# A state-space layer and a gated feed-forward on one core: when one tile is split, when four scalings run, and how two blocks of results are stored

## The chip, the core and the metric

The kernel runs on one core of one Trainium2 chip. The core's engines each work through a queue of their own: TensorE (PE; its weight loads are listed as PEld), VectorE (DVE), ScalarE (ACT), GpSimd (POOL) and SyncE (SP), which here does nothing but issue transfers. ACT issues a few transfers as well. Engines wait for each other by semaphores, and each works strictly in its queue's order. The metric is the device time of one launch in microseconds (us); less is better. Before the change it is 934.74 us (median of three runs, 934.41 to 935.01).

## The reference

Input `A_u` is x, 2048 tokens by 640 channels. A modulation vector gives two triples of shift, scale and gate. The first half adds a gated long convolution (a diagonal state-space layer, 128 states for each channel) of the normalized x; the second half adds a gated SwiGLU feed-forward with 1728 hidden units. Cut to the part that the change touches:

```
mod = (silu(c) @ w_mod).reshape(1, 6, 1, 640)
sa, ca, ga, sb, cb, gb = ...                     # shift, scale, gate, twice
x = x + ga * ssm(layernorm(x) * (1 + ca) + sa)   # first 480 us or so of the kernel
h = layernorm(x) * (1 + cb) + sb
x = x + gb * ((silu(h @ w1) * (h @ w3)) @ w2)    # the rest
```

Everything is fp32. The kernel multiplies in TensorE with operands that are split into a high part (rounded) and a low part (the remainder), three products for one: high by high, high by low, low by high.

## The kernel before

**Tiles.** The tokens are four blocks of 512 (b = 0 to 3), a token's place in a block being a partition and one of four columns j. The hidden units are fourteen tiles m of 128; tile 13 has only 64, and is handled as 64 rows of high part with 64 rows of low part below them in one operand. `self.H` is the order in which the late stretches take the tiles: 13, 0, 1, ..., 12.

**Stages of the feed-forward.** Blocks are worked in pairs, p = 0 (blocks 0 and 1) and p = 1 (blocks 2 and 3). `groups(p, ...)` makes, for each tile m, gate and up projections of both blocks with a scheme that saves one product in eight, the SiLU gate, and for the even block at once the down projection (`down`, L968), added up in five PSUM banks `acc0` to `acc4`. The odd block's hidden tiles stay in SBUF, in `self.h`. `late(p, ...)` then follows: it finishes the even block (b = 2p) and runs the down projection of the odd block (b = 2p + 1) over all fourteen tiles, 15 matmuls of 512 columns for each (10 for tile 13).

**What a tile of `late` needs.** Its down weights `w` (high and low, 640 KB) come by SP from the scratch tensor `w2d` (L750) into three buffers, so the load for a tile can be issued only when the tile three places earlier is done with. Its hidden tile is split by `hidden_split` (L820): ACT copies the high part to `ah` (L601), DVE subtracts it for the low part `al` (L602), two buffers of each. PE takes high products first, and meets `al` as the third matmul of a tile.

**The even block's end.** ACT reads the five banks to `oc` (`gated`, L991). For k = 0 to 3 DVE multiplies each `oc` with the row of gates `gbrow` (L1002) and adds it to x (`token_add`, L1013); for k = 4 PE turns it to tokens (`to`) and DVE adds it (L1009). Then SP stores the block in four transfers of 320 KB, one for each 32 partitions (`store`, L1021). The calls are spread over the loop by the table `extra` (`at(...)`), but the tile framework's scheduler, which simulates the program as it builds it, decides in which order instructions stand in each engine's queue.

**Between the pairs.** At the end of `late(0)`, `plain(2, ...)` and `plain(3, ...)` make hidden tile 13 of blocks 2 and 3: products in bank `gh`, then ACT (tanh `th` L956, copy L957) and DVE (L958, and L959 that reads the bank for the last time). Block 2's tile, `aa`, is split at once inside `plain` (ACT L828 and L829, DVE L830, result `ah`); it is the first operand that the next group's down projection takes. Block 3's goes to `self.h`. The first group of p = 1 needs PSUM banks out of the same three (`gu`), which `to` and the second `gh` still hold.

**The end.** In `late(1)` the last two tiles are taken bank by bank. DVE multiplies (L1511) and adds (L1013) row by row, and `store_row` (L1015) stores each finished row j of block 3 in four transfers of 80 KB, two from SP and two from ACT.

Of the kernel before, what the change touches and what calls it, by code (L numbers as in the profile page):

```python
# [10 lines left out]
F32 = mybir.dt.float32  # L11
F32R = mybir.dt.float32r
I32 = mybir.dt.int32
AF = mybir.ActivationFunctionType
ALU = mybir.AluOpType
# [5 lines left out]
D = 640  # L21
# [184 lines left out]
class K:  # L206
# [392 lines left out]

    def split(self, H, Lo, v, eng):  # L600
        self.nc.scalar.activation(H, v, AF.Copy)  # L601
        eng.tensor_tensor(Lo, v, H.bitcast(F32), op=ALU.subtract)  # L602

    def bank(self, name):
        return self.ps.tile([P, 512], F32, name=name, tag="gu", bufs=3)
# [211 lines left out]
        i = self.H.index(m)  # L817
        return self.xp.tile([P, 512], F32, name=f"h{m}", tag="ha", bufs=4) if i >= 10 else self.fp.tile([P, 512], F32, name=f"h{m}", tag="hb", bufs=10)

    def hidden_split(self, b, m, a, eng):  # L820

        A = self.nc.scalar
        ah, al = (self.fp.tile([P, 512], F32R, name=f"a{x}{b}_{m}", tag=f"a{x}", bufs=2) for x in "hl")
        if m < 13:
            self.split(ah, al, a, eng)
            return ah, al
        th = self.tmp(f"t{b}_{m}")
        A.activation(ah[:64], a[64:], AF.Copy)  # L828
        A.activation(th[64:], ah[:64].bitcast(F32), AF.Copy)  # L829
        self.nc.vector.tensor_sub(ah[64:], a[64:], th[64:])  # L830
        return ah, None
# [99 lines left out]
    def plain(self, b, X, tiles):  # L931

        nc = self.nc
        A, V = nc.scalar, nc.vector
        out = []
        gu = []
        for f, W in tiles:
            if f == 13:
                gu.append((f, [(self.bank(f"gh{b}"), lambda k, W=W: [t[:, k % 2] for t in W[k // 2]])]))
            else:  # L940
                gu.append((f, [(self.bank(f"gu{b}{i}"), lambda k, i=i, W=W: [t[:, i if k == 4 else k % 2] for t in W[4 if k == 4 else 2 * i + k // 2]]) for i in range(2)]))
        for k in range(KT):
            x = list(self.x_of(X, b, k))
            for _, pg in gu:
                for g, w in pg:
                    self.three(g, w(k), x, k == 0, k == KT - 1)
        for f, pg in gu:
            th = self.tmp(f"th{b}{f}")
            g = pg[0][0]
            a = self.tmp(f"aa{b}{f}") if b % 2 == 0 else self.h_tile(f)  # L950
            if f < 13:
                A.activation(th, g, AF.Tanh, scale=0.5)
                V.scalar_tensor_tensor(a, th, 1.0, g, op0=ALU.add, op1=ALU.mult)
                V.tensor_mul(a, a, pg[1][0])
            else:
                A.activation(th[64:], g[:64], AF.Tanh, scale=0.5)  # L956
                A.activation(a[64:], g[:64], AF.Copy)  # L957
                V.scalar_tensor_tensor(a[64:], th[64:], 1.0, a[64:], op0=ALU.add, op1=ALU.mult)  # L958
                V.tensor_mul(a[64:], a[64:], g[64:])  # L959
            if b % 2:  # L960
                self.h[f] = a
            else:
                out.append(self.hidden_split(b, f, a, V))
        return out

    def accumulators(self, b):
# [2 lines left out]
    def down(self, acc, m, a, w, start, stop, ks=range(KT)):  # L969

        (ah, al), (w2h, w2l) = a, w
        wide, rest = slice(0, 4 * P), slice(4 * P, D)
        for k in ks:
            sl = slice(k * P, (k + 1) * P)
            terms = [(ah, w2h), (ah, w2l), (al, w2h)][:3 if m < 13 else 2]
            for i, (x, y) in enumerate(terms):
                last = stop and i == len(terms) - 1
                if k < 4:
                    self.pe.matmul(acc[k], x[:, sl], y[:, wide], start=start and i == 0, stop=last)
                else:  # L980
                    self.pe.matmul(acc[k], y[:, rest], x, start=start and i == 0, stop=last)

    def gate_row(self):

# [11 lines left out]
            self.nc.scalar.activation(oc, acc[k], AF.Identity, scale=self.cols[:, 2, k:k + 1])  # L996
        return oc

    def output(self, b, oc, k):

        if k < 4:
            self.nc.vector.tensor_mul(oc, oc, self.gbrow)  # L1002
            self.token_add(b, oc, k)
            return
        pt = self.bank(f"to{b}{k}")
        for j in range(4):
            self.pe.transpose(pt[:, j * P:(j + 1) * P], oc[:, j * P:(j + 1) * P], self.ident)
        xs = self.x2[b][:, :, k * P:(k + 1) * P]
        self.nc.vector.tensor_add(xs, pt.rearrange("p (j d) -> p j d", j=4), xs)  # L1009
# [3 lines left out]
        self.nc.vector.tensor_add(xs, oc, xs)  # L1013

    def store_row(self, b, j):  # L1015
        for q in range(4):
            (self.nc.scalar if q % 2 else self.nc.sync).dma_start(self.ov[q, :, b * 4 + j, :], self.x2[b][q * 32:(q + 1) * 32, j, :])

    def store(self, b, d0=0, d1=D, qs=range(4), other=None):
        for q in qs:  # L1020
            (other if other and q > 1 else self.nc.sync).dma_start(self.ov[q, :, b * 4:b * 4 + 4, d0:d1], self.x2[b][q * 32:(q + 1) * 32, :, d0:d1])  # L1021

    H = (13, 0) + tuple(range(1, 13))

# [12 lines left out]
    def tail_tasks(self, border, border2, cut):  # L1037
# [237 lines left out]
        def gates(b, m, banks, n, last, names, r):  # L1275
# [47 lines left out]
            def down():  # L1323
                if m == 0:
                    self.acc = self.accumulators(0)
                self.down(self.acc, m, (t[4], t[5]) if m < 13 else t[6], (w2[m][:, 0], w2[m][:, 1]), m == 0, False)
            add("dn" + n, "PE", 3.42 if m < 13 else 2.28, down, ["gl" + n, f"w2l{m}"] + {0: [f"v1.{k}" for k in range(KT)] + ["gm1.0", "gm1.13"], 13: ["dn0.0", "pq0.4"], 1: ["dn0.13"]}[m], r + 1, give=[("w2", f"w2h{m}")])
        n_of = lambda m: 2 if m < 13 else 1
        plain(0, (0, 13), "pp0.", 17, [])
        plain(1, (0, 13), "pp1.", 33, [f"v1.{k}" for k in range(3)], True)  # L1330
        load_up(1)
        load_down(1)
        used = [f"pp1.{x}" for x in (1, 3, 1, 3, 4)]
        raw_split(1, 34, used)
        down_split(1, 52)
        plain(0, (1,), "pq0.", 35, ["pp1.4"])
        plain(1, (1,), "pq1.", 36, ["pq0.4"])
        load_up(2)
# [51 lines left out]
    H = (13, 0) + tuple(range(1, 13))  # L1390
# [46 lines left out]
    def late(self, p, acc, pend):  # L1437

        nc = self.nc
        b = 2 * p + 1  # L1440
        n = len(self.H)
        w2 = {i: self.w2_get(b, self.H[i]) for i in range(2)}
        X, v, xn = {}, {}, {}

        def hidden(i):
            return self.hidden_split(b, self.H[i], self.h.pop(self.H[i]), nc.vector)
        a = hidden(0)
        self.down(acc, *pend, True)
        oc = [self.gated(2 * p, acc, k) for k in range(KT)]
        acc = self.accumulators(b)  # L1450

# [8 lines left out]
        def at(i, f, *a):  # L1460
            extra.setdefault(i, []).append((f, a))
        for k in range(KT):
            at((k + 1) // 2, lambda k=k: self.output(2 * p, oc[k], k))
        for q in range(4):
            at(3 + 2 * q, self.store, 2 * p, 0, D, (q,))
        box = {}
        if p == 0:
            at(1, norm, 0)
# [22 lines left out]
        last = n - 2 if p else n  # L1491
        for i, m in enumerate(self.H[:last]):
            if i + 2 < n:
                w2[i + 2] = self.w2_get(b, self.H[i + 2])
            nxt = hidden(i + 1) if i + 1 < last else None
            self.down(acc, m, a, w2.pop(i), i == 0, i == n - 1)
            a = nxt
            for f, args in extra.get(i, ()):
                f(*args)
        if p:  # L1500
            keep = [(self.H[i], hidden(i), w2.pop(i)) for i in range(last, n)]
            for k in (4, 0, 1, 2, 3):
                for m, a, w in keep:
                    self.down(acc, m, a, w, False, m == self.H[-1], [k])
                if k == 4:
                    oc = self.gated(b, acc, k)
# [9 lines left out]
        oc = [self.gated(1, acc, k) for k in range(KT)]  # L1516
        a, = self.plain(2, X, [(13, box["half"])])
        self.output(1, oc[0], 0)
        self.output(1, oc[1], 1)
        self.plain(3, X, [(13, box["half"])])  # L1520
        _, part, W, _ = box["W"]
        for j in (5, 2, 6):
            part(j)
# [662 lines left out]
```

## Time and profile before

| Quantity | Before |
|---|---|
| Time, median of three runs | 934.74 us |
| Profiled execution, its own time | 935.07 us |
| Its span, first to last instruction | 933.3 us |
| PE busy | 854.7 us, 92% |
| DVE busy | 683.3 us, 73% |
| ACT busy | 542.7 us, 58% |
| POOL busy | 347.2 us, 37% |
| Mean granted TensorE clock | 0.986 of full speed |
| Moved by transfers | 127.40 MB, 137 GB/s on average |

The span is what instructions of the program cover; 1.8 us of the execution lie around it. Times in the profile are microseconds from the start of the span. A row of the timeline has the start, the length, the engine (SPq or ACTq where it only issues transfers), the line, the operation, what it writes and reads, the shapes, how many it merges, and in brackets how long the engine stood idle before it and whom it waited for. A helper hides many lines: nearly all of PE stands at L152.

### The profile page before, as it was taken

What the parts mean: (1) busy time and instruction counts of PE and PEld (TensorE: products, weight loads), DVE (VectorE), ACT (ScalarE), POOL (GpSimd) and SP (SyncE); (2) the same over time, 40 slices, a digit from 0 to 9 for tenths busy, and PEclk for the clock granted to TensorE, in tenths of its full rate; (3) what the DMA queues carried; (4) which work ended last, traced back from release to release, by engine and by line L of the source; (5) the groups of instructions that cost most, each with busy time, mean ns of one, the idle gap of its engine ahead of it and who ended that gap; (6) DMA issues with size and microseconds to landing.
All of it is one profiled execution on the core that took longest, in us unless ns stands there. A gap on an engine that the chain in (4) does not pass through costs nothing.

```text
span 933.3 us, 21092 instructions
## 1 busy us (share of the span) xinstructions
PE 854.7 (92%) x8317; PEld 677.6 (73%) x8317; DVE 683.3 (73%) x1238; ACT 542.7 (58%) x1037; POOL 347.2 (37%) x378
## 2 busy tenths in 40 slices
PE   1267999999999996999999999999999999999997
PEld 1035857877888883787777778878788888888776
DVE  7998999999989976797676775668656464646523
ACT  6689989989787743854444454446444443434311
POOL 0899989998999510002111111000121212120000
PEclk9997999999999998999999999999999999999999
DMA  9876563524143598755444412285522222220274
GB/s 205 263 237 173 161 154 106 141 70 128 48 116 85 141 219 232 171 186 178 147 122 127 142 58 80 77 251 176 160 89 85 85 85 85 85 85 29 94 244 142
DMA packets 110252, 127.40 MB, mean 137 GB/s; under 512 B 10825, under 2 KB 89929, under 8 KB 108873
## 3 DMA queue, kind: packets, MB, share of 16 engines
q1 hardware_dynamic: 108920, 125.01, 46.5%
q8 instruction: 65, 1.06, 0.5%
q10 hardware_dynamic: 1232, 1.05, 0.4%
q14 instruction: 35, 0.28, 0.1%
HBM read 95.89 MB, written 30.15 MB: 135 GB/s over the span
## 4 chain that ended last, share of the span: by engine, by line
PE 72%; DVE 12%; ACT 5%; DMA 5%; POOL 3%; issue 2%; SPq 1%; ACTq 0%; DVEq 0%; POOLq 0%
PE c L152 19%; PE acc L152 17%; PE X L152 12%; PE ps L152 5%; PE fz L152 4%; PE kps L152 3%; PE fk L152 3%; PE fh L152 3%; PE gu L152 3%; DVE xb L152 1%; DVE yy L152 1%; PE iy L152 1%; DMA zd<-zp 1%; DMA hs<-hb 1%; DVE xx L152 1%
## 5 line engine op out<-in xcount | busy, mean ns | idle before, releaser
L152 PE MATMUL acc<-w,ah 128*128 128x512 f32 x448 | 137.0, 391 | 0.9 <-DMA w<-w2d 0.9
L152 ACT ACTIVATE tr<-ph 128x512 f32<-128x512 int32 (+1 forms) x160 | 93.7, 599 | 7.0 <-DVE yy L152 3.9
L152 PEld LDWEIGHTS acc<-w,ah 128*128 128x128 f32 x448 | 83.4, 188 | 18.2 <-ACT ah L601 1.3
L602 DVE TENSOR_TENSOR wl<-s,wh 128x256 fp32r<-128x256 f32 x92 | 39.0, 424 | 68.1 <-ACT wh L601 68.0
L778 POOL TENSOR_TENSOR s<-wr 128x256 f32<-128x256 f32 x22 | 16.5, 751 | 179.4 <-DVE wl L602 84.0
L152 PE MATMUL acc<-w,al 128*128 128x512 f32 x208 | 81.2, 391 | 2.0 <-DVE al L602 2.0
L601 ACT ACTIVATE wh<-s 128x256 fp32r<-128x256 f32 x92 | 37.8, 410 | 76.7 <-PE X L152 56.0
L152 POOL TENSOR_TENSOR ph<-p,p 128x1024 int32<-128x1024 int32 x40 | 78.7, 1968 | 4.5 <-ACT tr L152 4.0
L601 ACT ACTIVATE wh<-wr 128x256 fp32r<-128x256 f32 x92 | 38.3, 418 | 52.6 <-PE X L152 39.7
L779 POOL TENSOR_TENSOR s<-s,wr 128x256 f32<-128x256 f32 x22 | 16.6, 754 | 128.2 <-issue 127.4
L839 ACT ACTIVATE t<-g 128x512 f32<-128x512 f32 x44 | 27.8, 631 | 53.9 <-DVE g L803 53.9
L152 DVE TENSOR_TENSOR yy<-yy,tr 128x512 f32<-128x512 f32 (+1 forms) x60 | 56.7, 947 | 2.6 <-ACT tr L152 1.5
L808 DVE SCALAR_TENSOR_TENSOR g<-t,g 128x512 f32<-128x512 f32 x48 | 33.7, 702 | 30.8 <-ACT t L839 28.9
L152 DVE TENSOR_TENSOR xx<-tr,xx 128x512 f32<-128x512 f32 x80 | 54.4, 684 | 2.3 <-ACT tr L152 1.8
L152 PE MATMUL fz<-fp,wz 64*128 64x512 f32 x224 | 53.9, 607 | 0.4 <-DVE fp L152 0.4
L152 PE MATMUL kps<-yy,xx 128*32 128x64 f32 x1920 | 37.1, 228 | 18.3 <-DVE xx L152 15.7
L152 PEld LDWEIGHTS kps<-yy,xx 128*32 128x32 f32 x1920 | 32.1, 113 | 27.6 <-issue 10.6
L602 DVE TENSOR_TENSOR wl<-wr,wh 128x256 fp32r<-128x256 f32 x92 | 40.5, 441 | 13.5 <-ACT wh L601 13.5
L152 PE MATMUL ps<-wk,xb 128*64 128x128 f32 x640 | 47.3, 294 | 2.8 <-DVE hb L152 0.9
L152 PEld LDWEIGHTS acc<-w,al 128*128 128x128 f32 x208 | 39.0, 188 | 11.1 <-DVE al L602 2.9
L152 PEld LDWEIGHTS ps<-wk,xb 128*64 128x64 f32 x640 | 43.2, 219 | 5.3 <-DVE hb L152 1.2
L780 POOL TENSOR_TENSOR s<-wr 128x256 f32<-128x256 f32 x22 | 16.9, 768 | 80.2 <-PE gu L152 48.8
(468 smaller groups left out, 2469.0 us busy)
## 6 DMA issues: line engine op xcount, KB each, us to landing
w<-w2d SPq DMA_DIRECT2D x42, 640.0 KB, 4.0
wr<-in_w SPq DMA_DIRECT2D x50, 320.0 KB, 3.7
w2d<-w SPq DMA_DIRECT2D x14, 640.0 KB, 3.8
zd<-zt SPq DMA_DIRECT2D x32, 256.0 KB, 3.0
xs<-in_x SPq DMA_DIRECT2D x16, 320.0 KB, 12.0
hs<-hb SPq DMA_DIRECT2D x20, 256.0 KB, 3.5
xb<-hs SPq DMA_DIRECT2D x20, 256.0 KB, 4.7
iz<-zd SPq DMA_DIRECT2D x32, 160.0 KB, 4.3
```

The costliest lines, as they stand in the source:

```text
L152: self.prev = self.k.order(f(*a, **kw), self.prev)
L601: self.nc.scalar.activation(H, v, AF.Copy)
L602: eng.tensor_tensor(Lo, v, H.bitcast(F32), op=ALU.subtract)
L778: eng.tensor_tensor(s[0], u[:, 0:2], u[:, 2:4], op=ALU.add)
L779: eng.tensor_tensor(s[1], s[0], g[:, 0:2], op=ALU.subtract)
L780: eng.tensor_tensor(s[2], g[:, 0:2], u[:, 0:2], op=ALU.subtract)
L808: V.scalar_tensor_tensor(g, th, 1.0, g, op0=ALU.add, op1=ALU.mult)
L839: tanh = lambda o, i: A.activation(o, i, AF.Tanh, scale=0.5)
```

## The change

Four edits, all in and around `late`.

- `plain` no longer splits block 2's tile 13; `late` does it after `plain(3)`, and the first copy (L828) gets a dependency on `gated13`, the last gate product of block 3.
- In `late(1)` the split of tile 0 (`early`) is written ahead of the reading of the banks, and the multiplications with `gbrow` for k = 1 to 3 get a dependency on its low part (`low`, that is `al`).
- In `late(1)` the four stores of block 2 get a dependency on the last matmul of the tile of the loop at which they are called (tiles 2, 4, 6 and 8), so one goes after each of these.
- `store_row` stores a row in two transfers of 64 partitions, one from SP and one from ACT, in place of four of 32.

`later` adds a dependency that the data does not ask for. Nothing of the arithmetic changes.

```diff
-    def hidden_split(self, b, m, a, eng):
+    def hidden_split(self, b, m, a, eng, then=None):
...
         if m < 13:
-            self.split(ah, al, a, eng)
+            self.lowest = self.split(ah, al, a, eng)
             return ah, al
         th = self.tmp(f"t{b}_{m}")
-        A.activation(ah[:64], a[64:], AF.Copy)
+        ins = A.activation(ah[:64], a[64:], AF.Copy)
+        if then is not None:
+            self.later(ins, then)
...
-                V.tensor_mul(a[64:], a[64:], g[64:])
+                self.gated13 = V.tensor_mul(a[64:], a[64:], g[64:])
...
-                out.append(self.hidden_split(b, f, a, V))
+                out.append(a)
...
-            self.nc.vector.tensor_mul(oc, oc, self.gbrow)
+            ins = self.nc.vector.tensor_mul(oc, oc, self.gbrow)
+            if then is not None:
+                self.later(ins, then)
...
-        for q in range(4):
-            (self.nc.scalar if q % 2 else self.nc.sync).dma_start(self.ov[q, :, b * 4 + j, :], self.x2[b][q * 32:(q + 1) * 32, j, :])
+        for q in range(2):
+            (self.nc.scalar if q else self.nc.sync).dma_start(self.ov[2 * q:2 * q + 2, :, b * 4 + j, :], self.x2[b][q * 64:(q + 1) * 64, j, :])
...
+    def later(self, ins, then):
+        self.tc.add_manual_dep(ins.ins, then.ins.name, mybir.DependencyInfo(mybir.DependencyClass.Sync, mybir.DependencyReason.DATA), reason="pace")
...
         a = hidden(0)
         self.down(acc, *pend, True)
+        early = hidden(1) if p else None
+        low = self.lowest if p else None
...
-            at((k + 1) // 2, lambda k=k: self.output(2 * p, oc[k], k))
+            at((k + 1) // 2, lambda k=k: self.output(2 * p, oc[k], k, low if k else None))
         for q in range(4):
-            at(3 + 2 * q, self.store, 2 * p, 0, D, (q,))
+            at(3 + 2 * q, lambda q=q: self.store(2 * p, 0, D, (q,), done if p else None))
...
-            nxt = hidden(i + 1) if i + 1 < last else None
-            self.down(acc, m, a, w2.pop(i), i == 0, i == n - 1)
+            nxt = (early if p and i == 0 else hidden(i + 1)) if i + 1 < last else None
+            done = self.down(acc, m, a, w2.pop(i), i == 0, i == n - 1)
...
         self.plain(3, X, [(13, box["half"])])
+        a = self.hidden_split(2, 13, a, nc.vector, self.gated13)
```

What this makes of the queues is seen at three places. The first is ACT between the pairs, from the copy of block 2's tile 13 on (`ah_13` and `t_13` are its split, `th` and `h` the gates of block 3, `wh` high parts of weights, `g_0` and `t_0` the next group's gate). Before:

```order
L828 ACTIVATE ah_13_8286<-aa_8281 64x512
L601 ACTIVATE wh_10_8326<-s_0_8016 128x256
L829 ACTIVATE t_13_8288<-ah_13_8286 64x512
L956 ACTIVATE th_8312<-gh_8296 64x512
L957 ACTIVATE h_8313<-gh_8296 64x512
L601 ACTIVATE wh_11_8373<-wr_1_8351 128x256
L838 ACTIVATE g_0_8371<-X_0_8364 128x512
L601 ACTIVATE wh_11_8390<-wr_1_8351 128x256
```

The same stretch of ACT's queue in the changed kernel:

```order
L601 ACTIVATE wh_10_8326<-s_0_8016 128x256
L958 ACTIVATE th_8306<-gh_8290 64x512
L959 ACTIVATE h_8307<-gh_8290 64x512
L601 ACTIVATE wh_11_8373<-wr_1_8351 128x256
L601 ACTIVATE wh_11_8390<-wr_1_8351 128x256
L828 ACTIVATE ah_13_8312<-aa_8281 64x512
L831 ACTIVATE t_13_8314<-ah_13_8312 64x512
L840 ACTIVATE g_0_8371<-X_0_8364 128x512
```

The split of tile 13 moved behind the gates of block 3 and two weight copies; the copy `g_0` of the next group stays behind it. DVE changes likewise: its subtraction for `ah_13` moved from ahead of block 3's gates to behind them and two low parts of weights, and the add of `to` (L1009, now L1014) moved behind one low part.

The second place is DVE at the start of `late(1)` (`oc` are the four results of block 2, `x_5403` its block of x, `al_0` to `al_1` low parts of tiles 0 and 1). Before:

```order
L1002 TENSOR_TENSOR oc_10185<-oc_10185,gbrow 128x512
L1002 TENSOR_TENSOR oc_10187<-oc_10187,gbrow 128x512
L1002 TENSOR_TENSOR oc_10189<-oc_10189,gbrow 128x512
L1002 TENSOR_TENSOR oc_10191<-oc_10191,gbrow 128x512
L1013 TENSOR_TENSOR x_5403<-oc_10185,x_5403 128x512
L602 TENSOR_TENSOR al_0_10203<-h_8487,ah_0_10202 128x512
L1013 TENSOR_TENSOR x_5403<-oc_10187,x_5403 128x512
L1013 TENSOR_TENSOR x_5403<-oc_10189,x_5403 128x512
L1013 TENSOR_TENSOR x_5403<-oc_10191,x_5403 128x512
L602 TENSOR_TENSOR al_1_10221<-h_8630,ah_1_10220 128x512
```

The same stretch of DVE's queue in the changed kernel:

```order
L1005 TENSOR_TENSOR oc_10189<-oc_10189,gbrow 128x512
L1018 TENSOR_TENSOR x_5403<-oc_10189,x_5403 128x512
L602 TENSOR_TENSOR al_0_10186<-h_8487,ah_0_10185 128x512
L1005 TENSOR_TENSOR oc_10191<-oc_10191,gbrow 128x512
L1005 TENSOR_TENSOR oc_10193<-oc_10193,gbrow 128x512
L1005 TENSOR_TENSOR oc_10195<-oc_10195,gbrow 128x512
L1018 TENSOR_TENSOR x_5403<-oc_10191,x_5403 128x512
L602 TENSOR_TENSOR al_1_10221<-h_8630,ah_1_10220 128x512
```

Three multiplications moved from ahead of `al_0` to behind it, and two of the adds from ahead of `al_1` to behind it. ACT's queue has the same order at this place as before.

The third place is SP in `late(1)`, from the weights of tile 4 on. Before, the four stores of block 2 (`out`) stood together:

```order
L750 DMA w_4_10272<-w2d 128x1280
L1021 DMA out<-x_5403 32x2560 x4
L750 DMA w_5_10294<-w2d 128x1280
L750 DMA w_6_10315<-w2d 128x1280
L750 DMA w_7_10337<-w2d 128x1280
L750 DMA w_8_10358<-w2d 128x1280
```

In the changed kernel they stand apart, and each is followed by the load whose buffer comes free with the same matmul that the store now waits for:

```order
L750 DMA w_4_10272<-w2d 128x1280
L1026 DMA out<-x_5403 32x2560
L750 DMA w_5_10294<-w2d 128x1280
L750 DMA w_6_10315<-w2d 128x1280
L1026 DMA out<-x_5403 32x2560
L750 DMA w_7_10337<-w2d 128x1280
L750 DMA w_8_10358<-w2d 128x1280
L1026 DMA out<-x_5403 32x2560
```

PE's order is the same in both kernels from the first instruction to the last. On POOL two sums of tile 1 of p = 1 change places.

More of the change, by code (lines that the diff above doesn't have):

```diff
@@ L601, in split @@
         self.nc.scalar.activation(H, v, AF.Copy)
-        eng.tensor_tensor(Lo, v, H.bitcast(F32), op=ALU.subtract)
+        return eng.tensor_tensor(Lo, v, H.bitcast(F32), op=ALU.subtract)
     def bank(self, name):
@@ L978, in down @@
                 if k < 4:
-                    self.pe.matmul(acc[k], x[:, sl], y[:, wide], start=start and i == 0, stop=last)
+                    done = self.pe.matmul(acc[k], x[:, sl], y[:, wide], start=start and i == 0, stop=last)
                 else:
-                    self.pe.matmul(acc[k], y[:, rest], x, start=start and i == 0, stop=last)
+                    done = self.pe.matmul(acc[k], y[:, rest], x, start=start and i == 0, stop=last)
+        return done
     def gate_row(self):
@@ L997, in gated, with output @@
         return oc
-    def output(self, b, oc, k):
+    def output(self, b, oc, k, then=None):
         if k < 4:
-            self.nc.vector.tensor_mul(oc, oc, self.gbrow)
+            ins = self.nc.vector.tensor_mul(oc, oc, self.gbrow)
+            if then is not None:
+                self.later(ins, then)
             self.token_add(b, oc, k)
@@ L1015, in store_row, with store @@
     def store_row(self, b, j):
-        for q in range(4):
-            (self.nc.scalar if q % 2 else self.nc.sync).dma_start(self.ov[q, :, b * 4 + j, :], self.x2[b][q * 32:(q + 1) * 32, j, :])
-    def store(self, b, d0=0, d1=D, qs=range(4), other=None):
+        for q in range(2):
+            (self.nc.scalar if q else self.nc.sync).dma_start(self.ov[2 * q:2 * q + 2, :, b * 4 + j, :], self.x2[b][q * 64:(q + 1) * 64, j, :])
+    def store(self, b, d0=0, d1=D, qs=range(4), then=None):
         for q in qs:
-            (other if other and q > 1 else self.nc.sync).dma_start(self.ov[q, :, b * 4:b * 4 + 4, d0:d1], self.x2[b][q * 32:(q + 1) * 32, :, d0:d1])
+            ins = self.nc.sync.dma_start(self.ov[q, :, b * 4:b * 4 + 4, d0:d1], self.x2[b][q * 32:(q + 1) * 32, :, d0:d1])
+            if then is not None:
+                self.later(ins, then)
+    def later(self, ins, then):
+        self.tc.add_manual_dep(ins.ins, then.ins.name, mybir.DependencyInfo(mybir.DependencyClass.Sync, mybir.DependencyReason.DATA), reason="pace")
     H = (13, 0) + tuple(range(1, 13))
```

## The prediction

> **What bounds the kernel now.** I read the page first, then the chain of work that ended last, then the timelines of the places where the chain leaves PE. The page's shares of the chain:
>
> ```profile
> PE 72%; DVE 12%; ACT 5%; DMA 5%; POOL 3%; issue 2%; SPq 1%; ACTq 0%; DVEq 0%; POOLq 0%
> ```
>
> Where PE has no gap the time cannot move, since the change takes no matmul away. So the busy time by stretch comes next (length, then busy time and count for PE, PEld, DVE, ACT, POOL, then clock, DMA share, GB/s): between the pairs, the start of the last `late`, and the end.
>
> ```profile
> 668.60:678.50 9.90, 8.02 (x36) 6.09 (x35) 8.09 (x13) 5.26 (x11) 3.43 (x4) 1.00 0.57 132
> 877.40:899.70 22.30, 20.55 (x91) 16.06 (x89) 10.21 (x17) 5.79 (x10) 0.00 (x0) 1.00 0.72 230
> 923.40:933.30 9.90, 4.59 (x23) 3.49 (x21) 5.89 (x9) 0.00 (x0) 0.00 (x0) 0.89 0.48 132
> ```
>
> PE lacks 1.9, 1.75 and 5.3 us there, at a granted clock of 1.00 in the first two, so the clock has no part in it. All four edits fall into these stretches. Three pieces of the chain in order of time (start, length, what):
>
> ```profile
> 690.95 3.40 PE acc L152 x15
> ...
> 877.74 2.41 DVE oc L1002 x4
> ...
> 893.07 6.46 DMA w<-w2d
> ```
>
> A tile of 15 matmuls takes 3.40, so 0.227 a matmul. The last `late` leaves PE twice: for DVE's four scalings, and for a weight load of 6.46.
>
> **Scalings behind the low part.** PE, then DVE and ACT, at the start of the last `late`:
>
> ```profile
> 880.03 0.63 PE L152 MATMUL acc<-w,ah 128*128 128x512 f32 x2
> 881.40 0.50 PE L152 MATMUL acc<-w,al 128*128 128x512 f32 x1 [0.75 <-DVE al L602]
> 877.65 2.49 DVE L1002 TENSOR_TENSOR oc<-oc,gbrow 128x512 f32<-128x512 f32 x4
> 880.06 0.69 DVE L1013 TENSOR_TENSOR x<-oc,x 128x512 f32<-128x512 f32 x1
> 880.66 0.69 DVE L602 TENSOR_TENSOR al<-h,ah 128x512 fp32r<-128x512 f32 x1
> 878.18 0.65 ACT L601 ACTIVATE ah<-h 128x512 fp32r<-128x512 f32 x1
> ```
>
> After two high matmuls, 0.45, the low one was due at 880.48; it came at 881.40: **0.92 lost**. Three scalings of 0.60 leave the place ahead of `al`, which moves from 880.66 to about 878.97 (0.1 is given back, because the add now directly follows the scaling that it reads). Its high part is there at 878.83. It ends at 879.66, 0.8 ahead of need, so all 0.92 goes. The next low part has three scalings and one add ahead of it and ends near 882.7; PE needs it at 880.03 + 3.40 + 0.45 = 883.9. The adds that come later feed only the stores. Bounds: 0.92, or 0 if DVE comes another 1.7 later than this. I take 0.92.
>
> **Stores apart.** SP's issues, and what PE meets:
>
> ```profile
> 889.25 0.80 SPq L1021 DMA_DIRECT2D out<-x  x2
> 891.24 1.73 SPq L1021 DMA_DIRECT2D out<-x  x1
> 891.78 0.62 PE L152 MATMUL acc<-w,ah 128*128 128x512 f32 x2
> 898.36 0.39 PE L152 MATMUL acc<-al,w 128*128 128x512 f32 x1
> 899.67 0.47 PE L152 MATMUL acc<-w,ah 128*128 128x512 f32 x1 [0.92 <-DMA w<-w2d]
> w<-w2d SPq DMA_DIRECT2D x42, 640.0 KB, 4.0
> ```
>
> The load of tile 5 stands behind four stores, issued from 889.25 to 892.97, the last alone in 1.73. Its buffer was free when PE began tile 3, 891.78; it was issued at 893.07 and took 6.46, where the median of such loads is 4.0. PE's next matmul started 1.31 after the one before it instead of 0.23: **1.08 lost**. Now one store goes ahead of each of the loads of tiles 5, 7, 9 and 11. A load has two tiles, 6.80, from the release of its buffer to its use. Four stores and one load took from 889.25 to 899.53, 10.3; less 4.0 for the load, a store costs at most 1.6. Issuing a store and a load takes 0.4 and 0.1 after the release; with 4.0 and 1.6 that is 6.1, which leaves 0.7, four times over, and the 1.08 goes. Bounds: 1.08, or 0 if each of the four loads comes 0.27 late. I take 1.08, from the row nearest to it, the first two stores, which left SP after 0.4 each.
>
> [...]
>
> **Split behind the gates.** PE between the pairs, then DVE, ACT and POOL:
>
> ```profile
> 668.38 0.39 PE L152 MATMUL gh<-x8h,wl_u 128*128 128x512 f32 x1
> 670.82 0.50 PE L152 MATMUL c<-x1h,wh 128*128 128x512 f32 x1 [0.22 <-DVE late L1009]
> 674.82 0.47 PE L152 MATMUL c<-x2hT,wh 128*128 128x512 f32 x1 [1.66 <-DVE h L959]
> 676.28 0.39 PE L152 MATMUL acc<-w,ah 128*128 128x512 f32 x1
> 670.07 0.69 DVE L1009 TENSOR_TENSOR late<-to,late 128x512 f32<-128x512 f32 x1
> 671.22 1.12 DVE L830 TENSOR_TENSOR ah<-aa,t 64x512 fp32r<-64x512 f32 x1
> 672.27 1.23 DVE L958 SCALAR_TENSOR_TENSOR h<-th,h 64x512 f32<-64x512 f32 x1
> 673.53 0.42 DVE L602 TENSOR_TENSOR wl<-wr,wh 128x256 fp32r<-128x256 f32 x1
> 673.98 0.69 DVE L959 TENSOR_TENSOR h<-h,gh 64x512 f32<-64x512 f32 x1
> 669.57 0.63 ACT L829 ACTIVATE t<-ah 64x512 f32<-64x512 f32 x1
> 670.11 0.57 ACT L956 ACTIVATE th<-gh 64x512 f32<-64x512 f32 x1
> 670.59 0.58 ACT L957 ACTIVATE h<-gh 64x512 f32<-64x512 f32 x1
> 672.28 0.42 ACT L601 ACTIVATE wh<-wr 128x256 fp32r<-128x256 f32 x1 [0.18 <-PE c L152]
> 671.76 1.19 POOL L780 TENSOR_TENSOR s<-wr 128x256 f32<-128x256 f32 x1
> ```
>
> PE's `c` at 674.82 waits for the bank that DVE's L959 frees. Ahead of that stand the split's 1.12 on DVE, and on ACT its two copies of 0.63. Without them ACT goes on as soon as `gh` is done, 668.8: a weight copy to 669.0, `th`, and L957 ends near 670.1 instead of 671.17. DVE now has one more low part of 0.45 ahead of the `to` add, so that add ends at 671.2, and PE's first `c`, which takes its bank, slips from 670.82 to 671.3. The gate L958 starts at 671.1; as POOL still runs then, I leave it its 1.23. With 0.45 and 0.69 behind it, L959 ends at 673.5 and `c` can go at **673.65**, 1.17 earlier.
>
> Then the split itself is what comes late. The weight copy of 672.28, now ahead of it on ACT, waits for PE's slipped `c` and ends at 673.15. When L959 ends, the two copies run from 673.6 to 674.9, DVE's subtraction, at the 0.69 of L959, ends at 675.65, and PE's `acc` goes at **675.75**. Six `c` after 673.65 it was due at 675.0; before it came at 676.28. Gain **0.5**. Behind the split on ACT stands the copy `g_0`, which frees a bank; it ends near 675.4, and PE needs the bank after ten more matmuls, at 678.0. Bounds: 1.1 if L958 takes 0.69 because POOL's sums fall elsewhere; minus 0.5 if the subtraction and a copy each lose half a microsecond. I take 0.5.
>
> **Half rows.** The end, and the first row's transfer by stretch:
>
> ```profile
> 928.76 0.69 DVE L1013 TENSOR_TENSOR x<-oc,x 128x512 f32<-128x512 f32 x1
> 929.48 0.86 ACTq L1017 DMA_DIRECT2D out<-x  x2
> out<-x ACTq DMA_DIRECT2D x8, 80.0 KB, 2.4
> 926.20:927.00 0.80, 0.80 (x5) 0.64 (x5) 0.80 (x2) 0.00 (x0) 0.00 (x0) 1.00 0.92 202
> 927.00:927.50 0.50, 0.50 (x4) 0.42 (x3) 0.47 (x2) 0.00 (x0) 0.00 (x0) 1.00 0.92 333
> ```
>
> Of each pair, the second transfer is issued 0.43 after the first; that goes. But the first now moves 80 KB more: a load of 640 KB takes 4.0 and a store of 80 KB takes 2.4, so 1.6/560 a KB, 0.23. Net **0.2**; bounds 0 (the transfer engines are already 0.92 busy during a row) and 0.43.
>
> [...]
>
> **Sum.** 0.92 + 1.08 + 0.5 + 0.2 = 2.7. The profiled execution of 935.07 (a span of 933.3 and 1.8 around it) becomes 932.4. It lies 0.33 above the median of 934.74, and from the median I forecast **932.0**.
>
> **Rivals.** *Loads somewhat late.* If a store costs the whole 2.46 by which the load of tile 5 exceeded the median, a load lands 6.96 after the release, 0.16 late, four times: 932.7. If 0.27 late, 933.1. For it: the 6.46; against: that load had four stores ahead. *Loads very late, the slower case.* SP issues the store, or the load behind it, as it did the fourth store, in 1.73 instead of 0.4; then a load is 1.3 + 0.16 late, four times, 5.8: about 938. It ends above the time before from 0.7 a load. Against it: the first two stores, issued with one load in flight, took 0.4. *The gates are no gain:* what L959 gains the late split gives back: 932.5, or 933.0 with the half microsecond lost. For it: two of DVE's operations on 64 rows took 1.12 and 1.23 while POOL ran, and the third may. *Both halves of a row at the faster rate:* 0.80 becomes 0.5, another 0.3: 931.7. *The low part stays late,* because DVE waits for ACT where I see no wait: 932.9.
>
> **Chances.** Forecast, 931.4 to 932.5: 0.50. No gain from the gates: 0.18. Loads somewhat late, 932.5 to 933.8: 0.13. Faster rows: 0.10. Low part late: 0.03. Slower: 0.06. The range from 930.8 (the upper bounds of gates and rows, and the faster rate) to 933.8 leaves out the last and the ends of the others. A measurement of this kernel can tell about 0.2% from no change, 1.87 us. Below 932.87 lie the forecast, the faster rows and most of the second case: faster 0.73, same 0.21, slower 0.06.
>
> **What would show it.** Right: no wait for `al` at the first full tile of the last `late`; none for `w` from tile 5 on; PE's `c` near 673.7, and a wait under a microsecond for `ah` ahead of `acc`; one issue per queue straight after DVE's last add, and an end 3.6 after it. Wrong: waits for `w` at tiles 5, 7, 9 or 11, or issues of over a microsecond there (loads late); `acc` at 676.3 or later (no gain from the gates). A shift ahead of 668 would come from something that I have not seen.

## The result and the profile after

| | Before | After |
|---|---|---|
| Time, median (range), four runs each on one chip | 934.88 us (934.41 to 937.27) | 959.36 us (957.68 to 962.02) |
| Span of the profiled execution | 933.3 us | 957.5 us |
| DVE's last add ends | 929.45 | 930.79 |
| From there to the end of the span | 3.85 | 26.7 |

The changed kernel takes 1.0249 times as long, with a 95% interval of 1.023 to 1.0269. It is **2.5% slower**, where 0.3% faster was forecast, and 25.6 us beyond the upper end of the range. The last two lines of the table show where: nearly all of it comes after the last arithmetic instruction.

The profile of after, in the order in which that of before was read. First the chain's shares by engine:

```profile
PE 72%; DVE 8%; ACT 7%; DMA 4%; POOL 2%; issue 2%; SPq 0%; ACTq 0%; DVEq 0%; POOLq 0%
```

DVE's share fell from 12% to 8%, which is some 35 us, far more than the waits of about 1 us that the change aims at. In a kernel below that has only the new stores, and DVE's order of before, it is 7%. So these shares say nothing of the waits, and neither does ACT's rise from 5% to 7%. What they do say is that they add up to 95%, where those of before make 100: the chain ends with DVE's last add at 930.79, and the 26.7 us behind it are in nobody's share. So the next view is busy time by stretch, with the columns as in the prediction (length; PE, PEld, DVE, ACT, POOL; clock, DMA share, GB/s). The stretches are the one between the pairs, the start of the last `late`, and two from the end:

```profile
671.20:681.10 9.90, 8.49 (x37) 6.11 (x36) 8.25 (x13) 5.61 (x11) 3.38 (x4) 1.00 0.57 132
878.80:901.10 22.30, 22.22 (x100) 18.04 (x99) 11.35 (x18) 6.88 (x12) 0.00 (x0) 1.00 0.63 194
927.00:931.00 4.00, 2.34 (x11) 1.59 (x9) 3.69 (x6) 0.00 (x0) 0.00 (x0) 1.00 0.09 20
934.00:955.00 21.00, 0.00 (x0) 0.00 (x0) 0.00 (x0) 0.00 (x0) 0.00 (x0) 0.50 0.13 52
```

In the second row PE lacks 0.08 us of 22.3 where it lacked 1.75: both waits at the start of the last `late` are gone. In the last row nothing computes for 21 us (PE has no work there, so its clock of 0.50 has no part in it), and the DMA share is 0.13, two engines of sixteen, at 52 GB/s. The rows of the last block in flight are 1.31 MB, at 52 GB/s 25 us. Before, the same stores ran at 202 to 333 GB/s with a share of 0.92. The issues themselves are as forecast, one per queue straight after each of DVE's adds:

```profile
926.72 4.61 SPq L1022 DMA_DIRECT2D out<-x  x4
930.10 0.69 DVE L1018 TENSOR_TENSOR x<-oc,x 128x512 f32<-128x512 f32 x1
```

The chain from the last `late` on (start, length, what):

```profile
881.94 7.59 PE acc L152 x32
...
889.97 27.27 PE acc L152 x120
...
917.25 5.07 DMA w<-w2d
...
922.46 2.33 PE acc L152 x9
```

No DVE scaling and no load interrupts it until 917.25. There a wait stands that before had only as 0.22: the weights of tile 12, the last one. PE's rows around it, two of before and two of after:

```profile
920.61 0.39 PE L152 MATMUL acc<-al,w 128*128 128x512 f32 x1
921.06 0.70 PE L152 MATMUL acc<-ah,w 128*128 128x512 f32 x2
...
920.91 0.39 PE L152 MATMUL acc<-al,w 128*128 128x512 f32 x1
922.46 0.70 PE L152 MATMUL acc<-ah,w 128*128 128x512 f32 x2 [1.16 <-DMA w<-w2d]
```

**Time by stretch.** The code ahead of 662 us is the same, yet PE's first `gh` between the pairs starts at 661.80 before and 664.44 after, and between 660.79 and 664.44 in the eleven profiles of this study. So stretches are compared, not positions. From PE's first `gh` to the end of DVE's last add before takes 267.65 and after 266.35, **1.30 less**. From matmul to matmul: between the pairs 0.17 less, around the low part 1.00 less, around tile 5 1.17 less, around tile 12 1.04 more. What comes after the last add is 22.9 longer.

### The profile page after: what moved, and what is told of

Its sections match the earlier page's. It is cut to its first block, busy times and chain, and to the rows that moved or that the text cites. A ratio compares the mean times of both kernels' runs of the same rounds, so it can differ in the third digit from the quotient of the medians.

```text
span 957.5 us, 21081 instructions
## 1 busy us (share of the span) xinstructions
PE 856.8 (89%) x8317; PEld 679.9 (71%) x8317; DVE 683.8 (71%) x1238; ACT 542.8 (57%) x1037; POOL 347.6 (36%) x378
## 4 chain that ended last, share of the span: by engine, by line
PE 72%; DVE 8%; ACT 7%; DMA 4%; POOL 2%; issue 2%; SPq 0%; ACTq 0%; DVEq 0%; POOLq 0%
PE c L152 18%; PE acc L152 18%; PE X L152 12%; PE ps L152 5%; PE fz L152 4%; PE kps L152 3%; PE fk L152 3%; PE fh L152 3%; PE gu L152 3%; DVE xb L152 1%; ACT tr L152 1%; DVE yy L152 1%; DMA zd<-zp 1%; PE iy L152 1%; ACT hn L152 1%
```

## Experiments

Each is timed against before on the same chip, but not all on one chip: the median of before was 934.88 us beside after, 936.78 beside the next four kernels of the table, 936.19 beside the four behind them and 936.13 beside the last. So ratios are to be compared, and not medians. Because the start scatters, the table has two lengths of each profiled execution beside the time: from PE's first `gh` to the end of DVE's last add ("work"), and from there to the end of the span ("tail").

| Kernel | Median us | Ratio to before, 95% interval | Work | Tail |
|---|---|---|---|---|
| before | | | 267.65 | 3.85 |
| after | 959.36 | 1.023 to 1.0269 | 266.35 | 26.7 |
| quarter rows | 934.24 | 0.9962 to 0.9989 | 266.5 | 3.9 |
| half rows alone | 959.30 | 1.0221 to 1.0275 | 268.0 | 26.7 |
| whole row | 946.18 | 1.0084 to 1.0128 | 266.3 | 15.7 |
| half rows, one step | 933.74 | 0.9963 to 0.9993 | 266.3 | 4.35 |
| last store earlier | 933.04 | 0.9946 to 0.9975 | 265.25 | 3.8 |
| stores alone | 934.42 | 0.9955 to 0.9981 | 267.1 | 3.7 |
| scalings alone | 934.82 | 0.9967 to 0.9989 | 267.0 | 3.8 |
| gates alone | 936.20 | 0.9993 to 1.0016 | 268.1 | 3.8 |
| last store earlier, no gates | 934.59 | 0.9968 to 0.9994 | 265.45 | 3.85 |

### The row's stores: which transfers run on two engines

The theory put to the test was that the number of transfer engines follows from the slowest dimension of the destination's access pattern, that is its outermost one. A quarter row goes to 32 rows of one step. A half row goes to `ov[2q:2q+2, :, ...]`, which is 2 by 32 rows, so its slowest dimension is 2. The rivals were a slow store of 64 partitions as such, or one of the other three edits.

**Quarter rows**, the change with the old `store_row`:

```diff
-        for q in range(2):
-            (self.nc.scalar if q else self.nc.sync).dma_start(self.ov[2 * q:2 * q + 2, :, b * 4 + j, :], self.x2[b][q * 64:(q + 1) * 64, j, :])
+        for q in range(4):
+            (self.nc.scalar if q % 2 else self.nc.sync).dma_start(self.ov[q, :, b * 4 + j, :], self.x2[b][q * 32:(q + 1) * 32, j, :])
```

> The changed kernel with the old store of a row, four quarters of 32 partitions; the other three edits stay. Theory (a half row whose destination has two levels, 2 by 32, is moved by two of the sixteen transfer engines): the whole loss of the tail goes, 931.5 to 934 us. Rival (part of the loss is in the spread stores or in the order at the gates): it stays above 937 us.

Measured 934.24 us, ratio 0.9975 (0.9962 to 0.9989), tail 3.9. The 22.9 are gone, and the other three edits together are a small gain, about 0.25%.

**Half rows alone**, before with only the new `store_row` (the reverse of that diff):

> The kernel before with nothing but the new store of a row in two halves. Theory: the tail alone makes the loss, 957 to 961 us, with DMA share about 0.13 and 50 GB/s after the last matmul. Rival (the halves are slow only because the spread stores crowd the queues): close to 935 us.

Measured 959.30 us, ratio 1.0248, tail 26.7. This one edit is the whole loss.

**Whole row**, the change with one transfer per row, so that the destination's slowest dimension is 4:

```diff
-        for q in range(2):
...
+        (self.nc.scalar if j % 2 else self.nc.sync).dma_start(self.ov[:, :, b * 4 + j, :], self.x2[b][:, j, :])
```

> The changed kernel with one transfer of all 128 partitions for a row, its destination in levels of 4 by 32, from SP and ACT in turn. Theory (the slowest level sets how many engines move it): four engines, the 512 packets of 2560 B of the block at 0.102 us each over four engines are 13 us in place of 26, so 945 to 947 us, and a DMA share of 0.25. Rival (a larger transfer, or one over more partitions, is slower in itself): 958 us or more.

Measured 946.18 us, tail 15.7. Its windows, as above:

```profile
930.00:943.00 13.00, 0.00 (x0) 0.00 (x0) 0.00 (x0) 0.00 (x0) 0.00 (x0) 0.50 0.24 87
```

A share of 0.24 is four engines of sixteen. The larger transfer is the faster one here, so size is not what slows the half row.

**Half rows, one step.** Still two transfers of 64 partitions, one from each queue, but to 64 rows with one step between them. This kernel leaves out the right order of block 3: the same rows of the output are written, with each other's contents.

```diff
+        ov = self.out.rearrange("(p r) d -> p r d", p=64)
         for q in range(2):
-            (self.nc.scalar if q else self.nc.sync).dma_start(self.ov[2 * q:2 * q + 2, :, b * 4 + j, :], self.x2[b][q * 64:(q + 1) * 64, j, :])
+            (self.nc.scalar if q else self.nc.sync).dma_start(ov[:, q * NJ + b * 4 + j, :], self.x2[b][q * 64:(q + 1) * 64, j, :])
```

> The changed kernel with half rows of 64 partitions whose destination is one level of 64 with a single step; the rows of block 3 land in permuted places of the output. Theory: same bytes, same partitions, same queues, but sixteen engines, so 931.5 to 934 us, like quarters or up to 0.4 us better. Rival (64 partitions, or 160 KB from one queue, are slow in themselves): near 958 us.

Measured 933.74 us, ratio 0.9978 (0.9963 to 0.9993). Same partitions, same bytes, same queues as in the change, and the tail is 4.35 instead of 26.7. Its windows from the first row's stores to past the last's:

```profile
925.20:927.20 2.00, 2.00 (x11) 1.65 (x10) 1.93 (x3) 0.00 (x0) 0.00 (x0) 1.00 0.41 81
927.20:929.20 2.00, 0.60 (x3) 0.17 (x1) 1.97 (x3) 0.00 (x0) 0.00 (x0) 1.00 0.78 250
929.20:931.00 1.80, 0.00 (x0) 0.00 (x0) 0.05 (x1) 0.00 (x0) 0.00 (x0) 1.00 0.75 248
```

The rates are 52, 87 and 250 GB/s for a slowest dimension of 2, 4 and 64, at shares of 0.13, 0.24 and 0.78: in these runs the destination's shape decides. The records of landings in the traces point the same way without any rate. A half row of the change leaves three marks, one of them 1.0 to 1.6 us after the issue and the other two much later; a quarter row and a half row of one step leave sixteen each. That agrees with one mark for each of 2 and of 16 engines, beside the early one, whose cause is open. The last kernel also gives the forecast's own term a fair trial. The transfer lists of the quarter rows, and then of this kernel (line, engine, KB each, median us from issue to landing):

```profile
out<-x SPq DMA_DIRECT2D x8, 80.0 KB, 2.1
out<-x ACTq DMA_DIRECT2D x8, 80.0 KB, 2.4
```

```profile
out<-x SPq DMA_DIRECT2D x4, 160.0 KB, 2.8
out<-x ACTq DMA_DIRECT2D x4, 160.0 KB, 3.1
```

A half row lands 0.7 later than a quarter, where 0.23 was reckoned, and 0.43 of issue is saved; the tail is 0.4 longer than with quarters. So even at a share of 0.75 to 0.78 the half rows show no gain in the tail. The times of the two kernels, 934.24 and 933.74, don't tell them apart.

### The other three edits, one by one

**Last store earlier**: quarter rows, and the fourth store of block 2 called one round earlier.

```diff
-            at(3 + 2 * q, lambda q=q: self.store(2 * p, 0, D, (q,), done if p else None))
+            at((3, 5, 7, 8)[q] if p else 3 + 2 * q, lambda q=q: self.store(2 * p, 0, D, (q,), done if p else None))
```

> The changed kernel with quarter rows, and the fourth store of block 2 called a round earlier, at loop 8 instead of 9, so that it goes ahead of the load of tile 10 and no longer ahead of that of tile 11. Theory: the load of tile 12 is late because the fourth store and the load of tile 11 stand ahead of it, while the last two tiles, taken bank by bank, need it only three matmuls after that of tile 11. Then the wait for it (1.16) shrinks to 0.2, as before the change, tiles 10 and 11 get no wait over 0.3, and the time is 1 us below that of the quarter rows alone. Rival: that load is late because its buffer comes free late, whatever goes ahead of it: a wait of 1.1 stays and the time is the same. Second rival: the wait only moves to tile 10 or 11.

Work falls from 266.5 to 265.25, 1.2 less; the four kernels with the change's order of stores lie between 266.3 and 266.5, so this is clear of their scatter. The time is 933.04, ratio 0.9961 (0.9946 to 0.9975), an interval that overlaps that of the quarter rows. PE's rows at the start of tile 12 in this kernel:

```profile
918.17 0.39 PE L152 MATMUL acc<-al,w 128*128 128x512 f32 x1
918.41 0.70 PE L152 MATMUL acc<-ah,w 128*128 128x512 f32 x2
```

The next start comes 0.24 after the one before: no wait at all, less than the 0.22 that before had. Tiles 10 and 11 have none either; the chain runs through 147 matmuls without a break (`acc`, 33.77 us). The issues in the change that the theory blames are the fourth store and, behind it, the loads of tiles 11 and 12:

```profile
913.85 0.34 SPq L1026 DMA_DIRECT2D out<-x  x1
914.23 3.34 SPq L750 DMA_DIRECT2D w<-w2d  x2
```

There these two loads took 4.98 and 5.07; with the store a round earlier they take 4.00 and 3.77. The theory holds: the store ahead of tile 11's load made tile 12's late. In this kernel all three waits of the last `late` are gone. Its work and its median are the lowest of the study, though five other kernels have ratios with intervals that overlap its own.

**Stores alone**: before, with only the four stores put behind tiles 2, 4, 6 and 8.

```diff
-            at(3 + 2 * q, self.store, 2 * p, 0, D, (q,))
+            at(3 + 2 * q, lambda q=q: self.store(2 * p, 0, D, (q,), done if p else None))
```

> Before, with nothing but the four stores of block 2 put behind tiles 2, 4, 6 and 8. Theory: the wait for the weights of tile 5 goes (1.1 gained) and one for those of tile 12 comes (1.1 lost), so the time stays within 0.5 us of before. Rival: the new wait at tile 12 comes from the other edits, which let PE arrive earlier; then it is under 0.3 here and the time is 1.1 less.

The wait at tile 5 is gone, and PE's timeline of this kernel has one at tile 12:

```profile
921.62 0.70 PE L152 MATMUL acc<-ah,w 128*128 128x512 f32 x2 [0.73 <-DMA w<-w2d]
```

It started 0.89 late, 0.67 more than before, so the edit alone gives 0.4 in these two places and 0.6 in all. The theory holds in kind. The wait is smaller than 1.1 because the load of tile 12 took 4.65 here, against 5.07 in the change and 4.83 to 5.09 in the other three kernels with this order of stores; why is open. The rival has no part in it: the load's release and its use are both PE's, and 3.9 apart here as there. The measured ratio, 0.9968, is 3 us, more than the 0.6 of the profile. The start of the kernel, which scatters by as much, may hold the rest; no run shows it.

**Scalings alone**: before, with only the early split of tile 0 and the dependency of the scalings.

```diff
+        early = hidden(1) if p else None
+        low = self.lowest if p else None
...
-            at((k + 1) // 2, lambda k=k: self.output(2 * p, oc[k], k))
+            at((k + 1) // 2, lambda k=k: self.output(2 * p, oc[k], k, low if k else None))
...
-            nxt = hidden(i + 1) if i + 1 < last else None
+            nxt = (early if p and i == 0 else hidden(i + 1)) if i + 1 < last else None
```

> Before, with nothing but the split of tile 0 ahead and the three scalings behind its low part. Theory: the wait for the low part (0.75) goes, and the last late starts 0.95 us earlier against what comes ahead of it; the load of tile 5 is still late, by the same amount, so that the time is 0.95 less. Rival: its buffer comes free 0.95 earlier but the four stores do not, so that PE meets the load later by as much, the wait at tile 5 grows by 0.95, and nothing is gained.

The wait for the low part is gone, and the one at tile 5 is longer. The chain of this kernel, with the load of tile 5 and what PE does after it:

```profile
892.42 6.85 DMA w<-w2d
...
899.40 21.34 PE acc L152 x93
```

The load now takes 6.85 instead of 6.46, and PE starts 1.46 late instead of 1.08. Work is 0.6 less, two thirds of the 0.92. That lies between theory and rival in size, but the rival's mechanism is not in the trace. Counted from the first `gh`, the first of the four stores is issued at 226.41 where before had 227.45, and the load at 230.23 where before had 231.27: both come 1.04 earlier, as PE does. Only the load itself takes longer. In half rows alone, without this edit, it takes 6.76 and PE starts 1.38 late, so the 0.38 lost here may be scatter; whether the edit has a part in it is open.

**Gates alone**: before, with only tile 13 of block 2 split behind the gates of block 3.

```diff
-                out.append(self.hidden_split(b, f, a, V))
+                out.append(a)
...
+        a = self.hidden_split(2, 13, a, nc.vector, self.gated13)
```

> Before, with nothing but the split of block 2's tile 13 behind the gates of block 3. Theory, from the changed kernel's trace: PE's first matmul of a gate bank that waits for the last gate product comes earlier, but the high part that comes late takes nearly all of it back; the stretch between the pairs is 0.2 shorter and no time measured can tell. Rival, as predicted: 0.5 shorter. Second rival: nothing, or longer.

From the first `X` between the pairs to the even block's last gate 0.18 less, as the theory had it. This small gain is a steady one: from the first `gh` to the last group of nine `c`, the six kernels with this edit take 209.86 to 209.90, and the five without it 210.02 to 210.05. But work is 0.5 longer, because here the load of tile 5 came 1.73 late (chain: `892.15 2.05 SPq L1026`, then the load with 6.59). Half rows alone, whose code up to that place is that of before, had 1.38 there. So that wait varies by some tenths between kernels that share the four stores in a row, and its 1.08 is not a constant.

**Last store earlier, no gates**: the fastest kernel without the first edit, whose diff is the last one reversed.

> The best version so far (quarter rows, the fourth store a round earlier) without the first edit: block 2's tile 13 is split inside plain, as before the change. Theory: the wait of 1.82 ahead of the c that the last gate product frees comes back and those for the late high part and the slipped bank go, 0.19 in sum, so that the stretch from PE's first gh to the end is 0.2 longer than that of the best version (269.05), and the waits of the last late stay as they are there. Rival: the late split also delays something behind it that the waits of PE between the pairs do not show; then this version is as short or shorter.

Work is 265.45 against 265.25: 0.2 longer, as the theory had it, all of it between the pairs (210.05 against 209.86), and the waits of the last `late` stay away. The median is 1.5 above that of the kernel with the gates, but on another chip, and the intervals of the two ratios overlap. The profiled executions differ in the start too (first `gh` at 664.40 against 661.75); why is open.

## Why the prediction was wrong

**Half rows: the failed step.** The text reckoned "the first now moves 80 KB more", 1.6/560 us a KB, and bounded the term by 0 and 0.43. The step took for granted that a transfer twice as large uses the same engines. The destination went from 32 rows of one step to 2 by 32, and each half ran on two engines, the same two for both queues: a share of 0.13 for both together and not 0.25, beside 0.24 for a whole row of 4 by 32 and up to 0.78 for halves of one step. The term was -22.9, not 0.2. The bound was wrong too: "the transfer engines are already 0.92 busy during a row" was read as a limit that could only cap the gain, when it was the thing that could be lost. No rival let the half rows lose anything either; the chance of 0.06 for a slower kernel stood for late loads. The rival with both halves of a row at the faster rate was worked out from 202 and 333 GB/s alone, and no run shows it: the halves of one step moved 250 and 248 GB/s, in stretches of 2.0 and 1.8 us.

**Scalings: right.** 0.92 was forecast, the wait of 0.92 is gone, and the stretch is 1.00 shorter. Alone the work fell by 0.6, since the load of tile 5 took 0.39 longer there; whether through this edit is not shown.

**Stores apart: the wait at tile 5 right, tile 12 missed.** 1.08 was forecast for tile 5, and the stretch around it is 1.17 shorter; tiles 7, 9 and 11 have no wait, so both rivals with late loads are wrong at the places that they named. The failed sentence is "a load has two tiles, 6.80, from the release of its buffer to its use". That does not hold for tile 12. The last two tiles are taken bank by bank, so its weights are wanted three matmuls after tile 11 starts: issued at its release at 917.25, wanted at 921.14, 3.9 us in place of 6.8, and the load took 5.07. Net of both tiles the term was 0.1 instead of 1.08. With the last store a round earlier all of it is there.

**Split behind the gates: right in kind, 0.5 was 0.2.** The rows of after in which it went, DVE's, PE's and POOL's:

```profile
674.87 0.85 DVE L602 TENSOR_TENSOR wl<-wr,wh 128x256 fp32r<-128x256 f32 x1
675.75 0.69 DVE L961 TENSOR_TENSOR h<-h,gh 64x512 f32<-64x512 f32 x1
676.59 0.47 PE L152 MATMUL c<-x2hT,wh 128*128 128x512 f32 x1 [0.47 <-DVE h L961]
678.61 0.97 PE L152 MATMUL acc<-w,ah 128*128 128x512 f32 x3 [0.39 <-DVE ah L832]
674.25 1.19 POOL L781 TENSOR_TENSOR s<-wr,s 128x256 f32<-128x256 f32 x1
```

Less the 2.64 by which all is later, `c` goes at 673.95 for 673.65 forecast, and `acc` at 675.97 for 675.75. The low part between the two gates took 0.85, beside POOL's 1.19, where 0.45 was put in; the gate ahead of it gave 0.15 back. So `acc` goes 0.31 earlier than before, and 0.17 are left: after the wait its eight matmuls take 2.12, where before they had no wait and took 1.98.

Without the fourth edit, the half rows, and with the store moved, the four terms make 0.2 + 1.0 + 1.2 + 0 = 2.4, which is what the fastest kernel's work lost (267.65 to 265.25). Its profiled execution took 932.58, where the sum of the forecast came to 932.4: the forecast fits that kernel, not this one. Part of that fit is luck: its first `gh` stands at 661.75, as that of before does at 661.80, where other profiles have up to 2.6 more.

## What to carry to other kernels

Before transfers are merged, look at the outermost dimension of the destination as the merged transfer has it: here one of 2, in place of 32, took the stores from a DMA share of 0.92 and 202 to 333 GB/s to 0.13 and 52 GB/s with the bytes unchanged, and such a fall of the share is the sign. A slack of so many tiles is to be reckoned for each tile by itself, the first and the last ones above all, where the order of the loop changes. Ahead of a late transfer the gain from a wait that went is to be read from the stretch in which it stood: here the stretch was 1.0 shorter, while the next load's own time moved by some tenths from kernel to kernel.

## What was not expected of the hardware

- Two queues that store halves of one row share the same two transfer engines: 52 GB/s at a share of 0.13 for both together, against 87 at 0.24, four engines, and about 250 at 0.75 to 0.78 with one step over 64 rows.
- At that share of 0.75 to 0.78 a transfer of 160 KB still lands 0.7 us later than one of 80 KB (2.8 and 3.1 against 2.1 and 2.4).
- Eleven profiles that share the code of the first 660 us reach the same matmul between 660.79 and 664.44. The cause is open; it is more than the whole gain that was forecast, 2.7, so small terms were read from stretches of the trace and not from the times.
